# Sliding-window attention and a gated layer on one core: the branch around the fast path removed, q and k loaded ahead of the weights, another planned order

## The chip, the cores and the metric

One core of a Trainium2 chip runs the whole program. The metric is the device time of one execution in microseconds (us); the median of several runs counts, lower is better.

## The reference

```
scores = q @ k^T / sqrt(64)                      # 4 batches, 8 heads, 768 positions, head width 64
keep   = (key < n_sink) | (0 <= query - key < window)      # n_sink 4, window 128
a      = softmax(where(keep, scores, -1e9))
x      = (a @ v), heads side by side             # 3072 x 512
h      = x @ w_in                                # 512 x 2048
out    = (h * cos(h)) @ w_out                    # 2048 x 512, result 3072 x 512
```

q, k and v are fp32. The two weights come as fp64; the kernel turns each into two fp32r parts (`hi` and `lo`) and multiplies with both. `n_sink` and `window` are inputs of 64 bits, read at run time.

## The kernel before

The 3072 tokens are 12 chunks of 256 (`NT`); a chunk is two blocks of 128 queries. For each chunk and head, `banded_path` computes scores against the block before, the own block and eight sink columns, masks them (`mask`, L811), takes exponentials (`expo`, L820), normalises (`norm`, L840), transposes (`turn`, L900) and multiplies by v (`values`, L954). Pairs of heads are then split into `xhi` and `xlo` (`split_x`; the subtraction for `xlo` is L333). The dense part (`dense`) goes over each chunk in 8 slots of 256 of the 2048 columns: 24 matmuls into `h` (L372), the gate h*cos(h) on ACT and DVE (the last product is L399), its split into `ghi` and `glo` (L405, L411), and 12 matmuls into two accumulators (L420). The first three chunks (the first 256 tokens of three batches) need no sinks and take a shorter way for the attention, with q and k turned on PE (`pe_turn`, L708) into `tqe` and `tk`.

A weight arrives in 32 pieces of 128 x 512 fp64 (512 KB) through two buffers `raw`. `weight_piece` makes fp32 of each in three integer steps on DVE (L473, L479, L485), rounds it on ACT to the `hi` part (L506) and subtracts for the `lo` part on DVE or POOL (L509). Much later each piece is loaded again and `check_piece` notes whether any weight was too small for this way.

The order of the work is not written by hand. `Plan` collects steps with the engines that can do them, their dependencies, an estimated duration and a due time; `order` plays them through and appends each step to the list of the engine that is free first, and the lists are emitted as they stand. The table `C` holds the offsets of the due times (`WI`, `WO` for weights, `DQ` for q and k, `TH` for the first heads, and so on) and the handicaps with which DVE, POOL and ACT compete for the steps that several can do (`ALT`, `POOLPEN`, `POOLF`). `FILL` are 60 matmuls (L1194) without a use, put where PE has nothing due.

At the start, `setup` loads the two limits to all 128 partitions (`nw_i`, L231 and L232, on SP's queue), makes the identity, 11 warm-up products and, on DVE, both the two limits as floats (`neg`) and a `flag` that says whether they suit the banded path. The steps that the plan puts before `GATE` (5.4 us) are emitted there too. Then every engine loads `flag` and branches (L1391, L1392); inside the branch DVE makes the masks (L1244 to L1252) and the rest of the plan follows. After it the check is reduced on DVE, PE and DVE (L1262 to L1266) into `redo`, and every engine loads `redo` (L1395) and branches around the general path (L1396), which does the whole computation again when `redo` is set.

Of the kernel before, what the change touches and what calls it, by code (L numbers as in the profile page):

```python
# [27 lines left out]
    "ALT": 2.669, "BLF": -0.052, "CK": 27.435, "DA": -3.097, "DH": -2.747, "DM": -0.791, "DQ": 10.525, "DS": -2.397,  # L28
    "DV": 4.41, "DX": 7.018, "FILL": 60, "GHI": 2, "GLO": 2, "L": 1, "LAG": 4.21, "LEAD": 18.263, "NEH": 24,
    "NM": 1.373, "NW": 2.093, "NWF": 0.026, "PB": 5, "PEN": 10.744, "PL": 3, "POOLF": 0.675, "POOLPEN": 2.303,  # L30
    "PRE": 4.5, "R": 2, "RAW": 2, "SAME": 0.13, "SEM": 0.2, "SPE": 0.3, "STEP": 5.59, "T": 6.142, "TH": -1.227,
    "WARM": 11, "WI": -18.566, "WO": 7.302, "WS": 1.56, "WS2": -0.177, "WT": 2, "XV": 2,
}
GATE = 5.4
# [12 lines left out]
class Plan:  # L47
# [5 lines left out]
    def __init__(self):  # L53
        self.steps, self.bufs, self.port, self.ahead = [], {}, set(), set()
# [6 lines left out]
    def add(self, engines, fn, deps, prio, lat=0.0, table=None, port=False, ahead=False):  # L61
        self.steps.append((engines, fn, deps, prio, lat, table))
        if ahead:
            self.ahead.add(len(self.steps) - 1)
        if port:
            self.port.add(len(self.steps) - 1)
        return len(self.steps) - 1

    def order(self, gate=0.0):
# [21 lines left out]
        free = dict.fromkeys(ready, gate)  # L91
        free["SP"] = min(gate, 0.9)
        free["DVE"] = free["ACT"] = min(gate, C["PRE"])
# [8 lines left out]
        while left:  # L102
# [4 lines left out]
            for e, rs in ready.items():  # L107
# [3 lines left out]
                for i in rs:  # L111
                    engines, _, _, prio, _, tab = steps[i]
                    if now < gate - 1e-6 and e != "SP" and i not in self.ahead:
                        continue
# [53 lines left out]
        early = gate - 1e-6  # L168
        return [s for s in starts if s[0] < early], [s for s in starts if s[0] >= early]
# [3 lines left out]
def attn_moe_kernel(ctx, tc, q, k, v, n_sink, window, w_in, w_out, out):  # L173
# [46 lines left out]
    nw_i = cp.tile([P, 2, 2], I32, name="nw_i")  # L220
    nw4 = cp.tile([P, 2, 2], F32, name="nw4")
    neg3 = cp.tile([P, 3], F32, name="neg")
    neg, quarter = neg3[:, 0:2], neg3[:, 2:3]
    flag = cp.tile([1, 4], F32, name="flag")
# [4 lines left out]
    def setup():  # L229

        nc.sync.dma_start(out=nw_i[:, 0, :], in_=n_sink.unsqueeze(0).broadcast_to([P, 2]))  # L231
        nc.sync.dma_start(out=nw_i[:, 1, :], in_=window.unsqueeze(0).broadcast_to([P, 2]))  # L232
# [7 lines left out]
        nc.gpsimd.memset(redo, 1)  # L240
        nc.gpsimd.memset(xb, 0.0)

        with tc.tile_pool(name="warm", bufs=1, space=PSUM) as pool:
            warm = pool.tile([P, P], F32, name="warm")
            for _ in range(C["WARM"]):
                nc.tensor.matmul(out=warm, lhsT=ident, rhs=ident, start=True, stop=True)
# [7 lines left out]
        nc.vector.tensor_copy(out=nw4, in_=nw_i)  # L254
        nc.vector.tensor_tensor(out=lims[:, 0], in0=nw4[0:1], in1=lims[:, 0], op=ALU.is_ge)
        nc.vector.tensor_tensor(out=lims[:, 1], in0=nw4[0:1], in1=lims[:, 1], op=ALU.is_le)
        nc.vector.tensor_single_scalar(out=neg, in_=nw4[:, :, 0], scalar=0.0, op=ALU.is_lt)
        nc.vector.tensor_tensor(out=lims[:, 0], in0=lims[:, 0], in1=lims[:, 1], op=ALU.mult)
        nw_hi = nw4[:, :, 1]
        nc.vector.tensor_tensor(out=nw_hi, in0=nw_hi, in1=neg, op=ALU.add)  # L260
        nc.vector.tensor_reduce(
            out=flag[:, 0:1], in_=lims[:, 0].rearrange("p a b -> p (a b)"), axis=mybir.AxisListType.X, op=ALU.min
        )
        nc.vector.scalar_tensor_tensor(
            out=neg, in0=nw_hi, scalar=4294967296.0, in1=nw4[:, :, 0], op0=ALU.mult, op1=ALU.add
        )
        nc.vector.tensor_copy(out=flag.bitcast(I32)[:, 1:2], in_=flag[:, 0:1])
# [184 lines left out]
    def weight_piece(plan, prio, hi, lo, src, guard, first=False):  # L452
# [7 lines left out]
        else:  # L460
# [6 lines left out]
            last = add(dma(1), load, [r], -1000.0 if first else prio - C["LEAD"], lat=3.3)  # L467
# [27 lines left out]
            s1 = add((("DVE", dve(WP, True)),), shift, [last, bt], prio, port=True, ahead=True)  # L495
            s2 = add((("DVE", dve(WP)),), top, [s1], prio, port=True, ahead=True)
            s3 = add((("DVE", dve(WP)),), low, [s2], prio, port=True, ahead=True)
# [13 lines left out]
        s4 = add((("ACT", act(WP)),), round_hi, [last], prio, ahead=True)  # L511
# [74 lines left out]
    def emit(steps, before=None):  # L586
        with tc.manual_schedule():
            if before:
                before()
            for _, _, fn, e in steps:  # L590
                fn(engines[e])

    def banded_path():
# [126 lines left out]
        def early_tiles(e):  # L720
            env.tqe = ap.tile([P, 2, NT], F32, name="tqe", tag="plo")
            env.vp = [
                ap.tile([P, CB, 2 * D], F32, name="vpe", tag="vr"),
                xp.tile([P, CB, 2 * D], F32, name="vpo", tag="x", bufs=1),
            ]
            for odd in range(2):
                e.memset(env.tqe[64 - odd * 64 : 128 - odd * 64, odd], 0.0)
            e.memset(env.vp[0][:, :, D:], 0.0)
            e.memset(env.vp[1][:, :, :D], 0.0)
# [244 lines left out]
        blank = add([("POOL", 1.2)], early_tiles, early, 0.0)  # L974
        env.minus, bgt = buf("gt", 1), buf("gt", 1)
        bgt.users.append(add([("POOL", 0.4)], lambda e: e.memset(f32(gt), 0.0), [bgt], 0.0))
# [16 lines left out]
        def before_softmax(g, o):  # L993
            nonlocal first, vs_last
            t = head_time(g)
            if o.i0 == CB and o.h == 0:
                first = o
                bx, o.bt, btb, o.bv, o.bvs = buf("xq", 1), buf("ts", 1), buf("tk", 1), buf("xb", 1), buf("vs", 1)
# [5 lines left out]
                o.vt = add([("DVE", 1.1)], vs_parts(o), [i, o.bvs], t - T + 3.4, port=True)  # L1004
# [8 lines left out]
            if o.early:  # L1013
                if o.odd == 0:
                    bx, bb, o.btq = buf("xq", 1), buf("b3", 1), buf("tqe", 1)
                    src = lambda c: q[o.b, o.h + c, o.i0 * P : o.i0 * P + NT, :]
                    i = add(dma(2), load_natural(xq_t, src, CB), [bx], t - 8 * T + C["DQ"] + 0.4, lat=2.3)
# [13 lines left out]
                    i = add(dma(2), load_natural(xk_t, src, o.nkb), [bx], t - 7 * T + C["DQ"] + 1.2, lat=2.4)  # L1031
# [84 lines left out]
        def after_softmax(g, o):  # L1116
# [4 lines left out]
                dma(1), load_v(o), [bx] + ([blank] if o.early else []), t - 2 * T + C["DV"] + 3.2, lat=2.4  # L1121
# [88 lines left out]
        for m, (t, (ready, ss), piece) in enumerate(sorted(pieces, key=lambda w: w[0])):  # L1210
            i = weight_piece(plan, t, *piece, guard=False, first=m < C["PL"])
# [13 lines left out]
        nh = 0  # L1225
        for t, a, s in slots:
            hs = ("b4", "b2") if a < NE - 1 else ("b4", "b2", "b3")
# [5 lines left out]
        assert len(checked) == len(checks)  # L1233

        first_loads, steps = plan.order(GATE)
        emit(first_loads, setup)
        yield
# [5 lines left out]
        with tc.manual_schedule():  # L1243
            nc.vector.tensor_scalar(out=prev, in0=rel, scalar1=float(P), scalar2=wd_f, op0=ALU.add, op1=ALU.is_lt)  # L1244
            nc.vector.tensor_scalar(out=diag, in0=rel, scalar1=wd_f, scalar2=None, op0=ALU.is_lt)
            nc.vector.scalar_tensor_tensor(out=diag, in0=rel, scalar=0.0, in1=diag, op0=ALU.is_ge, op1=ALU.mult)
# [145 lines left out]
    with tc.If(banded > 0):  # L1392
        with ExitStack() as ctx2:
            next(fast)
# [35 lines left out]
```

## Time and profile before

| | us |
|---|---|
| median of 3 runs | 759.07 (758.25 to 761.2) |
| profiled execution: its own time | 757.07 |
| its span, first to last instruction | 755.2 |
| PE busy | 727.7 (96%) |
| DVE busy | 609.5 (81%) |
| ACT busy | 567.1 (75%) |
| POOL busy | 160.0 (21%) |

PE is the matrix engine, DVE the vector engine, ACT the scalar engine, POOL the GpSimd engine, SP the engine whose queue issues transfers. A busy share is a mean over the whole span. A line such as L372 is a line of the kernel before.

### The profile page before, as it was taken

How to read it: one execution, taken by the hardware profiler on the slowest of the kernel's cores; microseconds unless marked ns; L12 is line 12 of the kernel's file. 1: busy time of each engine (PE TensorE's matmuls, PEld its weight loads, DVE VectorE, ACT ScalarE, POOL GpSimd, SP SyncE). 2: the span in 40 equal slices, each digit the busy share in tenths (PEclk: the TensorE clock that was granted, in tenths of full speed). 3: DMA queues.
4: the chain of work that ended last, by engine and by line, in shares of the span. 5: the costliest groups of instructions: out<-in, count | busy, mean ns of one | idle time of the engine just before them, and what ended most of it. 6: DMA issues, size and time to landing. Idle time of an engine off the chain costs nothing.

```text
span 755.2 us, 15272 instructions
## 1 busy us (share of the span) xinstructions
PE 727.7 (96%) x4975; PEld 663.9 (88%) x4975; DVE 609.5 (81%) x1591; ACT 567.1 (75%) x1326; POOL 160.0 (21%) x246
## 2 busy tenths in 40 slices
PE   7779999999999999999999999999999999999996
PEld 7668888899899999999999989999999999999994
DVE  4889989868899898889989888888788998964432
ACT  2879884978868868788788787788798788784332
POOL 3210101310212243342222322221211131120000
PEclk8999999999999999999999999999999999999999
DMA  5675664322653574474475333232233233110000
GB/s 148 165 196 168 174 174 152 79 48 34 144 146 78 107 199 104 96 194 110 85 186 132 65 90 65 37 69 47 50 73 64 50 73 56 27 39 2 29 1 33
DMA packets 215673, 71.50 MB, mean 95 GB/s; under 512 B 204320, under 2 KB 204320, under 8 KB 215584
## 3 DMA queue, kind: packets, MB, share of 16 engines
q1 hardware_dynamic: 215584, 70.43, 39.1%
q8 instruction: 41, 0.67, 0.4%
q14 instruction: 48, 0.39, 0.2%
HBM read 64.10 MB, written 6.29 MB: 93 GB/s over the span
## 4 chain that ended last, share of the span: by engine, by line
PE 82%; DVE 7%; DMA 5%; ACT 3%; issue 1%; SPq 1%; DVEq 0%; ACTq 0%
PE h L372 32%; PE acc L420 31%; PE av L954 5%; PE tp L900 5%; PE s L798 4%; DMA raw<-in_moe_w_out_dram 1%; DMA xq<-in_q_dram 1%; DMA raw<-in_moe_w_in_dram 1%; PE av L930 1%; PE s L742 1%; PE gp L882 1%; ACT p L820 1%; DVE wt L479 1%; DVE wt L473 1%; DVE wt L485 1%
## 5 line engine op out<-in xcount | busy, mean ns | idle before, releaser
L372 PE MATMUL h<-xhi,whi_in 128*128 128x256 f32 x768 | 224.3, 292 | 0.0
L372 PE MATMUL h<-xlo,whi_in 128*128 128x256 f32 x768 | 216.9, 282 | 0.0
L372 PE MATMUL h<-xhi,wlo_in 128*128 128x256 f32 x768 | 216.7, 282 | 0.0
L420 PE MATMUL acc<-whi_out,ghi 128*128 128x512 f32 x384 | 156.2, 407 | 0.6 <-ACT raw L361 0.6
L372 PEld LDWEIGHTS h<-xhi,whi_in 128*128 128x128 f32 x768 | 145.9, 190 | 8.7 <-issue 0.3
L372 PEld LDWEIGHTS h<-xhi,wlo_in 128*128 128x128 f32 x768 | 146.0, 190 | 7.4
L420 PE MATMUL acc<-wlo_out,ghi 128*128 128x512 f32 x384 | 151.7, 395 | 0.1
L420 PE MATMUL acc<-whi_out,glo 128*128 128x512 f32 x384 | 150.6, 392 | 0.0
L372 PEld LDWEIGHTS h<-xlo,whi_in 128*128 128x128 f32 x768 | 145.8, 190 | 0.0
L811 DVE CUSTOM_DVE_ANT_0 p<-s,mk 128x264 f32<-128x264 f32 (+1 forms) x192 | 76.6, 399 | 27.7 <-PE s L798 20.9
L820 ACT ACTIVATE p<-p,st 128x264 f32<-128x264 f32 (+1 forms) x192 | 93.2, 487 | 0.6
L420 PEld LDWEIGHTS acc<-whi_out,glo 128*128 128x128 f32 x384 | 72.1, 188 | 16.4
L405 ACT CAST ghi<-r 128x512 fp32r<-128x512 f32 x96 | 59.2, 617 | 35.6 <-PE acc L420 33.5
L394 ACT ACTIVATE r<-r,neg 128x512 f32<-128x512 f32 x96 | 68.9, 723 | 21.7 <-DVE r L387 19.4
L420 PEld LDWEIGHTS acc<-whi_out,ghi 128*128 128x128 f32 x384 | 72.5, 189 | 5.4 <-ACT raw L361 0.8
L420 PEld LDWEIGHTS acc<-wlo_out,ghi 128*128 128x128 f32 x384 | 72.9, 190 | 5.0 <-DVE wlo_out L509 0.7
L411 DVE TENSOR_TENSOR glo<-r,ghi 128x512 fp32r<-128x512 f32 x76 | 54.9, 722 | 27.6 <-ACT ghi L405 26.8
L399 DVE TENSOR_TENSOR r<-h,r 128x512 f32<-128x512 f32 x96 | 65.0, 680 | 10.4 <-ACT r L394 10.2
L387 DVE SCALAR_TENSOR_TENSOR r<-h,yt 128x512 f32<-128x512 f32 x96 | 65.6, 683 | 5.6 <-ACT yt L381 3.3
L381 ACT ACTIVATE yt<-h 128x512 int32<-128x512 f32 x96 | 57.2, 595 | 10.6 <-PE h L372 9.4
L853 POOL TENSOR_TENSOR vr<-v,vr 128x192 fp32r<-128x192 f32 (+1 forms) x55 | 32.2, 586 | 144.8 <-ACT vr L848 132.6
L840 POOL TENSOR_SCALAR p<-p,st 128x264 f32<-128x264 f32 (+2 forms) x62 | 33.3, 550 | 139.0 <-DVE st L830 125.3
(132 smaller groups left out, 1405.0 us busy)
## 6 DMA issues: line engine op xcount, KB each, us to landing
raw<-in_moe_w_in_dram SPq DMA_DIRECT2D x32, 512.0 KB
raw<-in_moe_w_out_dram SPq DMA_DIRECT2D x32, 512.0 KB
xk<-in_k_dram SPq DMA_DIRECT2D x256, 48.0 KB
v<-in_v_dram SPq DMA_DIRECT2D x64, 96.0 KB
out_dram<-raw SPq DMA_DIRECT2D x24, 256.0 KB
xq<-in_q_dram SPq DMA_DIRECT2D x144, 32.0 KB
xq<-in_q_dram SPq DMA_DIRECT2D x24, 64.0 KB
xk<-in_k_dram SPq DMA_DIRECT2D x24, 64.0 KB
```

The source lines that it names most:

```text
L372: nc.tensor.matmul(out=o.h[:, t, :], lhsT=w[:, c, fs], rhs=xx[:, c, :], start=(c == 0 and n == 0), stop=(c == NC - 1 and n == 2),)
L381: nc.scalar.activation(out=yt, in_=o.h, func=AF.Copy, scale=INV2PI, bias=0.25)
L387: nc.vector.scalar_tensor_tensor(out=o.r, in0=o.h, scalar=INV2PI, in1=yt, op0=ALU.mult, op1=ALU.subtract)
L394: nc.scalar.activation(out=o.r, in_=o.r, func=AF.Sin, scale=TWOPI_DOWN, bias=quarter)
L399: nc.vector.tensor_tensor(out=o.r, in0=o.h, in1=o.r, op=ALU.mult)
L405: nc.scalar.copy(out=o.ghi, in_=o.r)
L411: e.tensor_tensor(out=o.glo, in0=o.r, in1=f32(o.ghi), op=ALU.subtract)
L420: nc.tensor.matmul(out=x.acc[j], lhsT=gg[:, t, j * P : (j + 1) * P], rhs=w[:, f, :], start=(f == 0 and n == 0), stop=(f == NFT - 1 and n = ...
L811: nc.vector.tensor_tensor_reduce(out=o.p[:, j, :w], in0=o.s_ps[j][:, :w], in1=masks[min(o.i0 + j, 2)][:, :w], op0=ALU.add, op1=ALU.min, sc ...
L820: nc.scalar.activation(out=o.p[:, j, :w], in_=o.p[:, j, :w], func=AF.Exp, bias=o.lead.st[:, 0, o.nth, j : j + 1], scale=-1.0, accum_out=o. ...
L900: nc.tensor.transpose(out=o.tp[:, n * P : (n + 1) * P], in_=o.p[:, i - o.i0, c0 : c0 + P], identity=ident)
L954: nc.tensor.matmul(out=dst, lhsT=lhs, rhs=rhs, start=(n == 0), stop=(n == len(seq) - 1), skip_group_check=True)
```

## The change

The branch on `flag` goes. The plan is one list again (`GATE`, `PRE` and the steps marked as ahead are gone), and the engines' first free times in it are five new numbers (`P0` to `S0`). The limits are loaded by ACT's queue into one partition, four steps there make them floats, and one product of a row of ones with them (`both`) puts them on 128 partitions; `neg` is copied from it. The test of the limits moves to `limits`, part of the step `again`, which stands in the plan near the end, takes in the reduced check and writes `redo`. The loads of the first q and k get due times ahead of the first weight pieces. The clears of `vs` and `gc` become steps of the plan. The table has new values throughout, so that the planner makes another order and another share-out between engines; the steps themselves are the same.

```diff
 C = {
-    "ALT": 2.669, "BLF": -0.052, "CK": 27.435, "DA": -3.097, "DH": -2.747, "DM": -0.791, "DQ": 10.525, "DS": -2.397,
...
+    "ALT": 2.676, "BLF": -0.126, "CK": 45.236, "DA": -4.303, "DH": -1.332, "DM": -0.747, "DQ": 9.553, "DS": -2.337,
...
-GATE = 5.4
...
-        nc.sync.dma_start(out=nw_i[:, 0, :], in_=n_sink.unsqueeze(0).broadcast_to([P, 2]))
-        nc.sync.dma_start(out=nw_i[:, 1, :], in_=window.unsqueeze(0).broadcast_to([P, 2]))
+        nc.scalar.dma_start(out=nw_i[:, 0, :], in_=n_sink.unsqueeze(0))
+        nc.scalar.dma_start(out=nw_i[:, 1, :], in_=window.unsqueeze(0))
...
+            for _ in range(C["WARM"]):
+                nc.tensor.matmul(out=warm, lhsT=ident, rhs=ident, start=True, stop=True)
+
+            nc.vector.tensor_copy(out=nw4, in_=nw_i)
+            nc.vector.tensor_single_scalar(out=low, in_=nw4[:, :, 0], scalar=0.0, op=ALU.is_lt)
+            nc.vector.tensor_tensor(out=low, in0=nw4[:, :, 1], in1=low, op=ALU.add)
+            nc.vector.scalar_tensor_tensor(
+                out=low, in0=low, scalar=4294967296.0, in1=nw4[:, :, 0], op0=ALU.mult, op1=ALU.add
+            )
+            nc.tensor.matmul(out=both, lhsT=ones, rhs=low, start=True, stop=True)
...
+            nc.vector.tensor_copy(out=neg, in_=both)
...
-            last = add(dma(1), load, [r], -1000.0 if first else prio - C["LEAD"], lat=3.3)
+            last = add(dma(1), load, [r], first if first else prio - C["LEAD"], lat=3.3)
...
+                    pq = t - 8 * T + C["DQ"] + 0.4 if g else C["LD"] - 2
+                    i = add(dma(2), load_natural(xq_t, src, CB), [bx], pq, lat=2.3)
...
+        def again(e):
+            limits()
...
+            nc.vector.scalar_tensor_tensor(
+                out=redo, in0=tmin[0:1, 1:2], scalar=-MIN_TOP * MIN_TOP, in1=flag, op0=ALU.is_gt, op1=ALU.max
+            )
...
-    fast = banded_path()
-    next(fast)
-    banded = nc.values_load(flag.bitcast(I32)[:, 1:2], min_val=0, max_val=1)
-    with tc.If(banded > 0):
-        with ExitStack() as ctx2:
-            next(fast)
+    with ExitStack() as ctx2:
+        banded_path(ctx2)
     again = nc.values_load(redo, min_val=0, max_val=1)
```

SP's list at the start, before (`nw_i` are the limits, `raw` the weight buffers, `xq` and `xk` those of q and k, `xb` and `v` those of v):

```order
L231 DMA nw_i<-in_n_sink_dram 128x2
L232 DMA nw_i<-in_window_dram 128x2
L465 DMA raw_70<-in_moe_w_in_dram 128x1024
L465 DMA raw_71<-in_moe_w_in_dram 128x1024
L700 DMA xq<-in_q_dram 128x2x64 x2
L700 DMA xk<-in_k_dram 128x2x64 x2
L635 DMA xb<-in_v_dram 8x4x64 x4
L1391 TENSOR_LOAD flag
```

SP's list at the start with the change:

```order
L701 DMA xq<-in_q_dram 128x2x64 x2
L701 DMA xk<-in_k_dram 128x2x64 x2
L468 DMA raw_70<-in_moe_w_in_dram 128x1024
L468 DMA raw_71<-in_moe_w_in_dram 128x1024
L682 DMA vpe<-in_v_dram 128x2x64
L682 DMA vpo<-in_v_dram 128x2x64
L636 DMA xb<-in_v_dram 8x4x64 x4
```

The limits have left SP's queue, q and k stand first, and no branch follows.

DVE's list with the change, from the limits to the first masked score (`sm` holds the limits as floats, `both` is the product, `mk` the masks; L814 and L476 to L488 are L811 and L473 to L485 before):

```order
L255 SCALAR_TENSOR_TENSOR sm<-sm 1x2
L261 COPY neg<-both 128x2
L1291 TENSOR_SCALAR mk<-yt,neg 128x128
...
L1299 TENSOR_SCALAR mk<-mk 128x648
L476 TENSOR_SCALAR wt_72<-raw_70 128x512
L814 ISA p_0_0_201,st_0_0_202<-s_0_0_0_196,mk 128x128
L814 ISA st_0_0_202 128x1
L482 SCALAR_TENSOR_TENSOR wt_72<-raw_70,wt_72 128x512
```

Before, the masks' nine steps stood behind the branch and among three steps of two weight pieces; now they are in a row, and one weight step stands between them and the first masked score.

SP's list at the end with the change:

```order
L682 DMA v_1_77<-in_v_dram 128x3x64
L1424 TENSOR_LOAD redo
L1424 ISA x2
L439 DMA out_dram<-raw_70 128x512
L439 DMA out_dram<-raw_71 128x512
L439 DMA out_dram<-raw_70 128x512
L439 DMA out_dram<-raw_71 128x512
L1425 COMPARE_AND_BRANCH
```

Before, the load of `redo` and its branch stood behind the last store and the end of the first branch's body; now the load is ahead of the last four stores.

## Rows read from the trace of the kernel before

**Rows 1.** The page: span, and PE's busy time, share and instructions.

```profile
span 755.2 us, 15272 instructions
...
PE 727.7 (96%) x4975; PEld 663.9 (88%) x4975; DVE 609.5 (81%) x1591; ACT 567.1 (75%) x1326; POOL 160.0 (21%) x246
```

**Rows 2.** Windows: from:to, length, busy us of each engine, clock, DMA share, GB/s.

```profile
0.00:15.15 15.15, 10.23 (x48) 10.07 (x49) 6.49 (x30) 2.90 (x5) 5.30 (x17) 0.79 0.46 123
...
60.00:100.00 40.00, 36.06 (x240) 32.05 (x239) 37.85 (x86) 37.24 (x88) 4.82 (x5) 1.00 0.61 170
0.00:100.00 100.00, 83.11 (x517) 73.53 (x518) 81.64 (x233) 73.14 (x197) 18.69 (x31) 0.95 0.61 169
100.00:150.00 50.00, 48.77 (x317) 43.84 (x316) 45.44 (x100) 37.22 (x80) 11.42 (x13) 1.00 0.48 134
...
100.00:745.00 645.00, 641.68 (x4448) 588.26 (x4447) 527.44 (x1357) 492.75 (x1128) 141.33 (x215) 1.00 0.37 84
745.00:755.20 10.20, 2.95 (x14) 2.11 (x12) 0.42 (x2) 1.17 (x2) 0.00 (x0) 0.89 0.18 61
```

**Rows 3.** Timeline of SP's queue: start, issue time, line, transfer.

```profile
1.18 0.42 SPq L232 DMA_DIRECT2D nw_i<-in_window_dram  x1
1.65 0.90 SPq L465 DMA_DIRECT2D raw<-in_moe_w_in_dram  x2
```

**Rows 4.** Timeline of DVE, first 16 us: start, duration, line, instruction, what it waited for.

```profile
6.00 0.17 DVE L254 CAST nw<-nw_i 128x4 f32<-128x4 int32 x1 [3.84 <-DMA nw_i<-in_window_dram]
...
7.51 0.43 DVE L473 TENSOR_SCALAR wt<-raw 128x512 int32<-128x512 int32 x1 [0.55 <-DMA raw<-in_moe_w_in_dram]
...
9.66 0.53 DVE L1244 TENSOR_SCALAR mk<-yt,neg 128x128 f32<-128x128 f32 x1 [0.31 <-DVE wt L473]
...
13.10 0.50 DVE L1252 TENSOR_SCALAR mk<-mk 128x648 f32<-128x648 f32 x1
15.15 0.29 DVE L811 CUSTOM_DVE_ANT_0 p<-s,mk 128x128 f32<-128x128 f32 x1 [1.56 <-PE s L742]
```

**Rows 5.** Timeline of PE, first 20 us: q's turn, first scores, ten fillers.

```profile
9.55 0.66 PE L708 MATMUL qk<-ident,xq 128*128 128x128 f32 x2 [3.56 <-DMA xq<-in_q_dram]
...
14.49 1.38 PE L742 MATMUL s<-tk,tqe 128*128 128x128 f32 x4
...
17.67 1.43 PE L1194 MATMUL idle<-gt 128*128 128x256 f32 x10
```

**Rows 6.** The end: last stores, window of 0.5 us, the SP queue's own waits.

```profile
747.13 1.69 SPq L436 DMA_DIRECT2D out_dram<-raw  x2
...
750.00:750.50 0.50, 0.00 (x0) 0.00 (x0) 0.00 (x0) 0.00 (x0) 0.00 (x0) 1.00 0.45 107
...
SPq L1396 <- SPq L1396: 3.1, 1, 3.1
SPq L1425 <- PEq L1425: 0.6, 2, 0.5
```

**Rows 7.** Groups by line on DVE: busy us, mean ns, idle before and its releasers.

```profile
L411 DVE TENSOR_TENSOR glo<-r,ghi 128x512 fp32r<-128x512 f32 x76 | 54.9, 722 | 27.6 <-ACT ghi L405 26.8
...
L840 DVE TENSOR_SCALAR p<-p,st 128x264 f32<-128x264 f32 (+2 forms) x80 | 30.0, 428 | 0.5
...
L333 DVE TENSOR_TENSOR xlo<-x,xhi 128x256 fp32r<-128x256 f32 x15 | 8.0, 533 | 1.3 <-ACT xhi L316 1.3
L509 DVE TENSOR_TENSOR wlo_in<-wt,whi_in 128x512 fp32r<-128x512 f32 x11 | 7.5, 683 | 0.9 <-ACT whi_in L506 0.8
```

**Rows 8.** Timelines of DVE and POOL around 44 us.

```profile
44.35 1.41 DVE L473 TENSOR_SCALAR wt<-raw 128x512 int32<-128x512 int32 x1 [0.99 <-DMA raw<-in_moe_w_in_dram]
...
44.21 1.26 POOL L509 TENSOR_TENSOR wlo_in<-wt,whi_in 128x512 fp32r<-128x512 f32 x1 [2.47 <-ACT whi_in L506]
```

**Rows 9.** Timeline of DVE: the gate steps of the sixth and thirteenth slot.

```profile
96.82 0.68 DVE L399 TENSOR_TENSOR r<-h,r 128x512 f32<-128x512 f32 x1
...
151.08 0.68 DVE L399 TENSOR_TENSOR r<-h,r 128x512 f32<-128x512 f32 x1
```

More of the change, by code (lines that the diff above doesn't have):

```diff
@@ L53, in __init__ @@
     def __init__(self):
-        self.steps, self.bufs, self.port, self.ahead = [], {}, set(), set()
+        self.steps, self.bufs, self.port = [], {}, set()
     def buf(self, tag, n):
@@ L59, in buf, with add @@
         return row[-1]
-    def add(self, engines, fn, deps, prio, lat=0.0, table=None, port=False, ahead=False):
+    def add(self, engines, fn, deps, prio, lat=0.0, table=None, port=False):
         self.steps.append((engines, fn, deps, prio, lat, table))
-        if ahead:
-            self.ahead.add(len(self.steps) - 1)
         if port:
@@ L67, in add, with order @@
         return len(self.steps) - 1
-    def order(self, gate=0.0):
+    def order(self, late=False):
         steps = self.steps
@@ L90, in order @@
         ready = {e: set() for e in ("PE", "ACT", "POOL", "DVE", "SP")}
-        free = dict.fromkeys(ready, gate)
-        free["SP"] = min(gate, 0.9)
-        free["DVE"] = free["ACT"] = min(gate, C["PRE"])
+        free = dict.fromkeys(ready, 0.0)
+        if late:
+            free.update(PE=C["P0"], ACT=C["A0"], DVE=C["D0"], POOL=C["G0"], SP=C["S0"])
         events = [(0.0, i) for i in range(n) if not wait[i]]
@@ L167, in order @@
                 now = wake[0]
-        early = gate - 1e-6
-        return [s for s in starts if s[0] < early], [s for s in starts if s[0] >= early]
+        return starts
 @with_exitstack
@@ L239, in setup @@
         nc.gpsimd.iota(rc_i[:, 1], pattern=[[1, P]], base=0, channel_multiplier=0)
-        nc.gpsimd.memset(redo, 1)
         nc.gpsimd.memset(xb, 0.0)
[L243 to L246, printed above, removed]
+        nc.vector.memset(ones, 1.0)
         nc.vector.memset(quarter, HALF_PI_DOWN)
@@ L253, in setup, with limits @@
         nc.vector.tensor_copy(out=rc, in_=rc_i)
[L254 to L260, printed above, removed]
+        with tc.tile_pool(name="warm", bufs=1, space=PSUM) as pool:
+            warm = pool.tile([P, P], F32, name="warm")
+            both = pool.tile([P, 2], F32, name="both")
+            for _ in range(C["WARM"]):
[7 more added lines that the diff above has]
+            nc.tensor.matmul(out=both, lhsT=ones, rhs=low, start=True, stop=True)
+            for _ in range(C["WARM2"]):
+                nc.tensor.matmul(out=warm, lhsT=ident, rhs=ident, start=True, stop=True)
+            nc.vector.tensor_copy(out=neg, in_=both)
+    def limits():
+        nc.vector.tensor_tensor(out=lims[:, 0], in0=nw4, in1=lims[:, 0], op=ALU.is_lt)
+        nc.vector.tensor_tensor(out=lims[:, 1], in0=nw4, in1=lims[:, 1], op=ALU.is_gt)
+        nc.vector.tensor_tensor(out=lims[:, 0], in0=lims[:, 0], in1=lims[:, 1], op=ALU.max)
         nc.vector.tensor_reduce(
-            out=flag[:, 0:1], in_=lims[:, 0].rearrange("p a b -> p (a b)"), axis=mybir.AxisListType.X, op=ALU.min
+            out=flag, in_=lims[:, 0].rearrange("p a b -> p (a b)"), axis=mybir.AxisListType.X, op=ALU.max
         )
[L264 to L267, printed above, removed]
     ns_f = neg[:, 0:1]
@@ L509, in rest_lo @@
             e.tensor_tensor(out=lo, in0=t32, in1=f32(hi), op=ALU.subtract)
-        s4 = add((("ACT", act(WP)),), round_hi, [last], prio, ahead=True)
+        s4 = add((("ACT", act(WP)),), round_hi, [last], prio)
         s5 = add(sub(WP), rest_lo, [s4], prio, port=True)
@@ L1003, in before_softmax @@
                 i = add(dma(4), load_batch_v(o), [o.bv], t - 3 * T, lat=2.3)
-                o.vt = add([("DVE", 1.1)], vs_parts(o), [i, o.bvs], t - T + 3.4, port=True)
+                d = [i, o.bvs]
+                held.append(d)
+                o.vt = add([("DVE", 1.5)], vs_parts(o), d, t - T + 3.4, port=True)
                 o.bv.users.append(o.vt)
@@ L1271, in banded_path @@
-        yield
+        for _, _, fn, e in steps:
+            fn(engines[e])
     def general_path():
@@ L1286, in general_path @@
         }
-        emit(plan.order()[1])
+        emit(plan.order())
         for a, (b, i0) in enumerate(chunks):
```

123 lines of the change are left out of this document (69 added, 54 removed).

## The prediction, made before the result was known

> **What bounds the kernel now.** I read the page first, then the windows by stage, then the timeline of the first 16 us engine by engine, the last 10 us, and last the groups of instructions that the change moves. The page [rows 1] shows PE busy 96% of the 755.2 us span. The windows [rows 2] say where the rest lies: from 100 to 745 us PE misses 645 - 641.68 = 3.3 us in all, and from 745 us on 10.20 - 2.95 = 7.3 us. The first 100 us miss 16.9 us, and there PE also runs 60 filler matmuls and 11 warm-up products that compute nothing. So the kernel is PE-bound in its long middle part, and can win only at its two ends, unless the middle gets worse.
>
> **The start.** SP issues the two limits, two weight pieces, then q and k [rows 3]. The limits' second transfer, issued at 1.18, releases DVE at 6.00 [rows 4], 4.8 us later; each limit goes to 128 partitions. PE gets q at 9.55 and its first scores at 14.49 [rows 5]. On DVE the mask steps begin at 9.66, behind the branch, and the last one starts at 13.10; the first masked score is at 15.15 [rows 4]. Up to there DVE was busy 6.49 us of 15.15 [rows 2], so idle 8.7.
>
> **The end.** The second of SP's last two stores is issued at about 748.4 (747.13 + 1.69 less 0.4 for its own issue), and the transfers are over in the window that begins at 750.0 [rows 6]; so a store takes 1.9 us. The span ends 4.9 us after 750.3. The queue's own waits there are 3.1 us on SP's own L1396, the branch over the general path, and 0.6 us in two pieces on L1425 [rows 6]; what is left, some 1.2 us, I read as the wait for all transfers, the load of `redo` and the compare, which stand in SP's order behind the last store.
>
> **The sum is made against** the profiled execution's own 757.07 us (span 755.2 and 1.9 around it), which is 2.0 us under the median of the runs, 759.07. I add those 2.0 at the end. A measurement of this kernel can tell about 0.5% (3.8 us) from no change.
>
> **The change, part by part.**
>
> *End: -2.5.* In the new order SP loads `redo` ahead of the last stores and has the compare right behind them, and the two steps that reduce the check stand before the last slots on DVE. The 1.9 us of the last store now lie beside the branch's 3.1, and the load and exit (some 0.6 of the 1.2) go. Bounds: 0, if the exit waits for the stores before it branches, and -3.7 (all of 1.9, 1.2 and 0.6). I take 1.9 + 0.6.
>
> *Start: -4.* First the chain. The limits go out on ACT's queue, the second at about 1.2, one partition each. The trace has no transfer that small; bounds are 4.8 us [rows 4] and 1.9 us (the store). I take 2.1, near the store, because the 128 targets are gone: landed at 3.3. Four steps on DVE, each about 0.1 us behind the one before, make 3.7; the product and the copy 0.6 more: 4.3. The nine mask steps took 13.10 + 0.50 - 9.66 = 3.9 us with three weight steps of 0.6 between them, so 2.1 without: 6.4. On PE the product at 4.0, 18 fillers at 0.14 each [rows 5] and the two turns of q and k put the first scores at about 7.5, if q and k, now first in SP's order, have landed by 4.6. DVE's first masked score stands behind the first step on a weight piece, whose transfer is issued at about 2.6 instead of 1.65 and took until 7.51 before [rows 4]; so about 8.2 for 15.15, 6.9 us earlier. DVE has done less by then (about 4.5 us of work for 6.49, as the two weight pieces are not yet begun), so its idle time falls from 8.7 to 3.7: 5.0 us saved. From there to 100 us DVE is nearly full (81.64 - 6.49 = 75.2 busy of 84.85) [rows 2], so it is DVE's work that paces PE until PE has a stock. Up to the sixth gate step L399, at 96.82 [rows 9], the new order has 2 `glo` and 4 `wlo` more on DVE (4.2 us at the means of [rows 7]), and 4 weight steps, 2 masks and 4 sink steps fewer: about 1 us less. So the sixth gate comes some 6 us earlier. Up to the thirteenth, at 151.08, it has 8 us more than before (4 `glo`, 8 `wlo`, 4 other steps of 2 us, less 6 `p` of 0.43); that is 9 us more between the two gates, against DVE's idle 50 - 45.44 = 4.6 us there [rows 2]. Of the 4.4 not covered I let half, 2, come through to PE. Hence -6 + 2 = -4. Bounds: -6.9 (the whole head start is kept) and -1.6 (all 4.4 comes through).
>
> *Middle: 0.* The new order takes work from POOL: on DVE's list there are 96 `glo` for 76, 30 `xlo` for 15, 31 `wlo` for 23, and 71 `p` for 80. At the means of [rows 7] that is 20 x 0.722 + 15 x 0.533 + 8 x 0.683 - 9 x 0.428 = 14.4 + 8.0 + 5.5 - 3.9 = 24 us more on DVE. From 100 to 745 us DVE is idle 645 - 527.44 = 117.6 us [rows 2], which covers it five times over, and nothing of it is a result that PE waits for on average; bounds are -3.3, all the idle time PE has left there, and +12, half of the 24 us. PE itself has the same matmuls in both orders.
>
> A row speaks for a lower price of the moved work. One weight step on DVE that takes 0.43 us at 7.51 [rows 4] took 1.41, from 44.35 to 45.76, while a subtraction on POOL ran from 44.21 to 45.47 [rows 8]: DVE stood until POOL was done. The Trainium skill, page "SBUF — State Buffer", section "Who interferes with whom", has this as a rule: the port pair that DVE and GpSimd share is an exclusive lock, held for a whole instruction. By that rule the 43 subtractions that leave POOL also stop blocking DVE, and the 24 us would be an upper price; by the rows alone it is 24, and the sum takes 0 in either case.
>
> *At nothing:* 5 warm-up products for 11 (PE idles there anyway); the two issues gone from SP (0.8 us, inside the head start); the clears of `vs` and `gc`, which POOL makes later, between two steps of its own that wait for DVE anyway.
>
> Sum: 757.07 - 2.5 - 4.0 + 0 = 750.6; with the 2.0 us to the median, **752.6 us**.
>
> **The rivals.**
>
> 1. *The head start is swallowed.* DVE's 9 us more between the sixth and thirteenth gates come through in full, and more idle time behind the first scores eats the rest: start 0, end -2.5: 756.6. For it speaks that DVE is busy 37.85 of the 40 us from 60 to 100 [rows 2]; against it that PE hardly waits after 100 us, when DVE still had idle time. Chance 0.15.
>
> 2. *The limits land late.* By the 4.8 us of [rows 4], now from 1.2 on: landed at 6.0, masks ready at 9.1 for 6.4, 2.7 us later; PE, too, stands behind the product, and the fillers are queued behind it. Start -1.3, so 755.3. The Trainium skill, page "SBUF — State Buffer", section "Can I just issue two DMAs to hit both halves?", says that issuing from several engines does not help, since all transfers share the same 16 engines. By that rule the other queue alone brings nothing, and only the single partition can. For it: q, k and weights are in flight at once. Against it: q and k are issued about when the limits are, not 1 MB of weights. Chance 0.12.
>
> 3. *DVE becomes the bound in the middle: slower.* Place: `glo`, `xlo` and the masks in the slots after 100 us. It decides if DVE's idle time there is mostly waiting on ACT and PE, which cannot be filled. Then a us more on DVE is a us on PE, and if more than 6.5 of the 24 come through, the kernel is slower; with all but the start's share, say 18, it is 757.07 - 6.5 + 18 + 2 = 770.6. Against it: 117.6 us of idle, and the same `wlo` subtraction takes POOL 1.26 us [rows 8] and DVE 0.683 [rows 7], so what waits on a moved one waits less. Chance 0.08.
>
> 4. *All of it is kept:* start -6.9, end -2.5, and 2 of PE's 3.3 us in the middle go too: 747.7. For it: weights are asked for earlier, and POOL blocks DVE less. Chance 0.17.
>
> That the change does not do what it says is hardly open: the branch is gone from every engine's list, and q and k stand first on SP's.
>
> **How the numbers follow.** The forecast has 0.48, with its own range from 749 to 755. Faster by over 0.5% means under 755.3: 0.46 of the forecast, all of rival 4, 0.07 of rival 2: 0.70. Slower means over 762.9: rival 3 and a rest, 0.09. Within 0.5%: 0.21. The range takes in rivals 4, 2 and 1 and leaves out rival 3 and the extremes: from 745 (all lower bounds at once give 757.07 - 3.7 - 6.9 - 3.3 + 2.0 = 745.2) to 757.5.
>
> **What would show it.** Right, if DVE's first masked score is near 8.2 (under 9), PE's first scores near 7.5, the sixth gate near 91, the last store issued some 4 us earlier, and the span ends about 2.4 us after that store has landed. Rival 2 shows as a first mask step after 6.5; rival 1 as PE idle of 17 us or more in the first 100 us; rival 3 as PE idle well over 3.3 us after 100 us, released by DVE. A tail as long as before, or more than 8 us of new PE idle in the middle, would make the prediction wrong.

## The result, and the profile after

The changed kernel takes 746.67 us (median of 4 runs, 746.09 to 748.58) against 759.73 beside it: ratio 0.9831, interval 0.9808 to 0.9853. In a later job, with its own variants around it, it took 748.49 against 759.64: 0.9861, 0.9840 to 0.9881. So it is faster by 11 to 13 us. The two profiled executions are 9.9 us apart in span, because the profiled execution of before lies below the median of its runs.

The page of the changed kernel, for [rows 1]:

```profile
span 745.3 us, 15192 instructions
...
PE 725.2 (97%) x4965; PEld 660.8 (89%) x4965; DVE 614.6 (82%) x1637; ACT 555.6 (75%) x1319; POOL 112.1 (15%) x201
```

The windows by stage, for [rows 2]; columns as there:

```profile
0.00:10.15 10.15, 8.54 (x37) 8.23 (x38) 4.31 (x24) 2.39 (x4) 2.32 (x13) 1.00 0.60 161
60.00:100.00 40.00, 37.92 (x257) 34.08 (x254) 38.88 (x97) 34.05 (x88) 4.35 (x7) 1.00 0.65 182
0.00:100.00 100.00, 88.34 (x557) 77.75 (x557) 86.88 (x248) 76.53 (x208) 10.25 (x25) 0.98 0.65 180
100.00:150.00 50.00, 49.08 (x319) 44.78 (x320) 45.00 (x103) 35.69 (x79) 3.30 (x9) 1.00 0.43 116
100.00:735.00 635.00, 632.72 (x4391) 579.95 (x4392) 527.74 (x1390) 477.89 (x1110) 101.83 (x177) 1.00 0.37 83
735.00:745.30 10.30, 4.16 (x19) 3.11 (x17) 0.00 (x0) 1.17 (x2) 0.00 (x0) 0.94 0.17 59
```

PE's idle time in the first 100 us falls from 16.9 to 11.7 us. Of its busy time there the warm-up takes 2.5 us for 4.6, and the 60 fillers take 11.8 in both; so PE has done 7.3 us more of useful work by 100 us. In the middle PE misses 2.3 us for 3.3. The tail is 1.2 us shorter (below). Together that is 7.3 + 1.0 + 1.2 = 9.5 of the 9.9; the other 0.4 is PE's busy time on the same useful products, which differs by that much between the two executions.

The start, for [rows 3 to 5]: the cast of the limits and the first masked score on DVE; on PE the product, the fillers behind q's turn, and the first scores:

```profile
2.66 0.22 DVE L252 CAST sm<-nw_i 1x4 f32<-1x4 int32 x1 [0.55 <-DMA nw_i<-in_window_dram]
...
10.15 0.29 DVE L814 CUSTOM_DVE_ANT_0 p<-s,mk 128x128 f32<-128x128 f32 x1 [2.63 <-PE s L745]
```

```profile
3.79 0.58 PE L258 MATMUL both<-sm,wt 1*128 1x2 f32 x2
...
5.92 1.84 PE L1213 MATMUL idle<-gt 128*128 128x256 f32 x7
...
9.48 1.21 PE L745 MATMUL s<-tk,tqe 128*128 128x128 f32 x4
```

DVE has its masks early, then waits 2.63 us for PE, and PE is at fillers, 0.26 us each. The first masked score comes 5.0 us sooner than at 15.15. The sixth and thirteenth gates, for [rows 9]:

```profile
87.42 0.67 DVE L402 TENSOR_TENSOR r<-h,r 128x512 f32<-128x512 f32 x1
...
146.25 0.69 DVE L402 TENSOR_TENSOR r<-h,r 128x512 f32<-128x512 f32 x1
```

They are 9.4 and 4.8 us sooner. A single gate is a rough measure, though: the eleventh is 3.4 us sooner and the twelfth 9. The twelfth, before and with the change:

```profile
146.84 0.68 DVE L399 TENSOR_TENSOR r<-h,r 128x512 f32<-128x512 f32 x1
```

```profile
137.79 0.69 DVE L402 TENSOR_TENSOR r<-h,r 128x512 f32<-128x512 f32 x1
```

The end, for [rows 6]: SP's last two stores, and two windows of half a microsecond:

```profile
738.45 1.69 SPq L439 DMA_DIRECT2D out_dram<-raw  x2
```

```profile
741.00:741.50 0.50, 0.00 (x0) 0.00 (x0) 0.00 (x0) 0.00 (x0) 0.00 (x0) 1.00 0.67 234
741.50:742.00 0.50, 0.00 (x0) 0.00 (x0) 0.00 (x0) 0.00 (x0) 0.00 (x0) 1.00 0.16 41
```

SP's load of `redo` and its branch over the general path in the kernel before (durations in ns, then the first and the last start in us):

```profile
L1395 SPq TENSOR_LOAD <-redo x1: 727/727/727, 749.1 to 749.1; - x1
L1396 SPq COMPARE_BRANCH  x1: 45/45/45, 749.9 to 749.9; - x1
```

The branch with the change, and what SP does next:

```profile
L1425 SPq COMPARE_BRANCH  x1: 45/45/45, 740.2 to 740.2; - x1
L1425 SPq EVENT_SEMAPHORE  x8: 17/17/17, 743.4 to 743.9; - x8
```

With the change SP comes to the branch at 740.2, as soon as the last store is issued (738.45 + 1.69 = 740.14), and goes on at 743.4. The stores are over by about 742, so they land beside the branch. Before, the load of `redo` stood between the last issue and the branch, and SP came to the branch at 749.9; the stores were over only by about 750.5 [rows 6], so there, too, they landed in part beside the branch. From the start of the last stores' issue to the branch it is 1.75 us for 2.8 before, from the branch to the end 5.1 for 5.3, in all 6.85 for 755.2 - 747.13 = 8.07.

DVE's groups that grew or got cheaper, for [rows 7]:

```profile
L414 DVE TENSOR_TENSOR glo<-r,ghi 128x512 fp32r<-128x512 f32 x96 | 66.3, 691 | 31.6 <-ACT ghi L408 31.2
...
L476 DVE TENSOR_SCALAR wt<-raw 128x512 int32<-128x512 int32 x32 | 13.5, 421 | 2.3 <-DMA raw<-in_moe_w_in_dram 2.1 <-DMA raw<-in_moe_w_out_dram 0.2
L336 DVE TENSOR_TENSOR xlo<-x,xhi 128x256 fp32r<-128x256 f32 x30 | 13.4, 446 | 1.1 <-ACT xhi L319 1.0
```

### The profile page after: what moved, and what is told of

Its sections match the earlier page's. It is cut to its first block, busy times and chain, and to the rows that moved or that the text cites. A ratio compares the mean times of both kernels' runs of the same rounds, so it can differ in the third digit from the quotient of the medians.

```text
span 745.3 us, 15192 instructions
## 1 busy us (share of the span) xinstructions
PE 725.2 (97%) x4965; PEld 660.8 (89%) x4965; DVE 614.6 (82%) x1637; ACT 555.6 (75%) x1319; POOL 112.1 (15%) x201
## 4 chain that ended last, share of the span: by engine, by line
PE 86%; DVE 6%; DMA 3%; ACT 3%; issue 1%; SPq 0%; POOL 0%; DVEq 0%; POOLq 0%; ACTq 0%
PE h L375 33%; PE acc L423 33%; PE av L957 5%; PE tp L903 5%; PE s L801 4%; DMA raw<-in_moe_w_in_dram 2%; PE av L933 2%; PE s L745 1%; PE idle L1213 1%; DMA xk<-in_k_dram 1%; PE gp L885 1%; DVE p L814 1%; DVE wt L482 1%; ACT p L841 1%; DVE wlo_in L512 1%
## 5 line engine op out<-in xcount | busy, mean ns | idle before, releaser
L814 DVE CUSTOM_DVE_ANT_0 p<-s,mk 128x264 f32<-128x264 f32 (+1 forms) x192 | 76.7, 400 | 23.2 <-PE s L801 17.3
L414 DVE TENSOR_TENSOR glo<-r,ghi 128x512 fp32r<-128x512 f32 x96 | 66.3, 691 | 31.6 <-ACT ghi L408 31.2
L843 POOL TENSOR_SCALAR p<-p,st 128x264 f32<-128x264 f32 (+2 forms) x70 | 36.1, 530 | 236.8 <-DVE st L833 202.5
L856 POOL TENSOR_TENSOR vr<-v,vr 128x192 fp32r<-128x192 f32 (+1 forms) x57 | 35.5, 623 | 183.4 <-ACT vr L851 148.0
```

The lines of the kernel that those rows point to most:

```text
L414: e.tensor_tensor(out=o.glo, in0=o.r, in1=f32(o.ghi), op=ALU.subtract)
L814: nc.vector.tensor_tensor_reduce(out=o.p[:, j, :w], in0=o.s_ps[j][:, :w], in1=masks[min(o.i0 + j, 2)][:, :w], op0=ALU.add, op1=ALU.min, sc ...
```

## The experiments

Every ratio is to the kernel before, run in the same job; 0.001 is 0.76 us.

**A later start in the same order.** Two kernels put more warm-up products ahead of the product of the limits, in an order otherwise the same.

```diff
-"WARM": 5,
+"WARM": 17,      (warm29: 29)
```

> The changed kernel with 17 warm-up products instead of 5, nothing else. They stand ahead of the product that spreads the limits; before, 11 of them took 4.63 us, so 12 more put everything behind the product (masks, fillers, scores) about 5.0 us later, in the same order. Theory A (the head start at the beginning passes to the end in full): 746.7 + 5.0 = 751.7. Theory B (the head start is mostly swallowed by DVE's work up to the thirteenth gate, the gain comes from the new order): under +2, at most 748.7.

> The changed kernel with 29 warm-up products instead of 5: 24 more, about 10.1 us later in the same order. Theory A: 756.8, a straight line through the 17 of the other run. Theory B: under +4, at most 750.7.

Measured: warm17 0.9855 (0.9833 to 0.9877), warm29 0.9886 (0.9867 to 0.9906). That is 1.8 and 4.2 us above the changed kernel's first ratio, 0.7 and 3.0 above the mean of its two. The doses were smaller than meant: the first masked score came 2.1 and 4.8 us later, for behind more warm-up products the fillers ran at 0.15 us each. The sixth gate came about 2.8 and 6.9 us later, the end of the profiled span 2.0 and 7.4 (warm29's profiled execution is the slowest of its six). The two doses against each other, in one job, are the cleanest pair: a start 2.7 us later makes a median 2.4 us later (750.28 and 752.69, each known to about 1.6). So in this order most of a late start seems to reach the end, as theory A had it.

**Structure and table apart.** `old_numbers` is the changed code with the old table (but 5 warm-up products, and with the numbers that only the new table has), `new_numbers` the code before with the new table (but 11). Six of the values that `old_numbers` puts back:

```diff
 C = {
-    "DA": -4.303, "DS": -2.337, "DV": 5.777, "DX": 5.639, "LEAD": 26.374, "WI": -20.327,
+    "DA": -3.097, "DS": -2.397, "DV": 4.41, "DX": 7.018, "LEAD": 18.263, "WI": -18.566,
...
```

> The changed kernel (no branch around the banded path, limits through ACT's queue and the product, q and k first, check ahead of the last slots), but with the old values of the table in all entries that both have, except the number of warm-up products. So the planner shares out and orders the work nearly as before, with the head start kept. Theory A (head start kept, order neutral): 746.7 within 2. The prediction's own sum (order neutral, 2 us given back) has 753. Theory B (the new order is what gains): 754 or more.

> The kernel before with the new table for every number that both tables have; the branch, the limits to 128 partitions ahead of the weights, q and k behind the weights, 11 warm-up products and the check at the end stay. Theory A (the new order hands a late or early start through one to one, as the warm-up doses showed): about 5 us of late first scores and 1.2 us of tail on top of the changed kernel, 753, ratio 0.990 to 0.994, the sixth gate about 5 us later than the changed kernel's 87.4. Theory B (the order alone is the gain, the start matters little): under 750, ratio under 0.986. Theory C (the order needs the early start, whose times its numbers were chosen for): 757 or more, ratio over 0.997.

| ratio to before | old numbers | new numbers |
|---|---|---|
| code before | 1 | 1.0008 (0.9989 to 1.0027) |
| changed code | 0.9961 (0.9941 to 0.9981) | 0.9831 and 0.9861 |

The changed code alone brings 3 us (1.4 to 4.5 by the interval) and takes 758.47 us, as theory B had it (754 or more); the table alone brings nothing, as theory C had it; together they bring 11 to 13. But each cell is one planned order, and the neighbours below show that a near order can cost 5 to 7 us. So the table does not show that code and numbers need each other. The old numbers in the changed code show one way in which a head start goes. Their first masked score is at 9.17, a microsecond ahead of the changed kernel, and their sixth gate at 96.12, where it was before. The window from 60 to 100 us, and DVE's waits from 55 to 125 us (engine, line, what for: us, times, longest):

```profile
60.00:100.00 40.00, 34.43 (x204) 30.14 (x203) 32.70 (x78) 29.72 (x71) 8.81 (x9) 0.91 0.55 161
```

```profile
DVE wt L475 <- DMA raw<-in_moe_w_out_dram: 3.4, 3, 1.2
...
DVE wt L475 <- DMA raw<-in_moe_w_in_dram: 1.2, 1, 1.2
```

DVE is busy 32.70 us there, 38.88 in the changed kernel, and waits 4.6 us for weights. PE falls behind too: from 70 to 75 us it is busy 2.59 us, and of the ten that follow a good part runs at 1.2 for 2.4 GHz (granted mean 0.66; 60 to 100 us in the changed kernel 1.00):

```profile
75.00:85.00 10.00, 9.22 (x45) 8.36 (x46) 7.71 (x17) 5.32 (x13) 2.17 (x2) 0.66 0.58 171
```

How much of the loss is the waits and how much PE's slower pace was not separated. In the changed kernel, whose `LEAD` is 8 us larger, the same wait for weights is one of 0.2 us:

```profile
DVE wt L476 <- DMA raw<-in_moe_w_out_dram: 0.2, 1, 0.2
```

`new_numbers` does not wait for weights there either, and its start is as late as before (first masked score at 15.31, sixth gate at 96.84); so weights in time are not enough by themselves.

**The branch alone.** The kernel before without the branch on `flag`, and so without the test of the limits.

```diff
-    banded = nc.values_load(flag.bitcast(I32)[:, 1:2], min_val=0, max_val=1)
-    with tc.If(banded > 0):
-        with ExitStack() as ctx2:
-            next(fast)
+    with ExitStack() as ctx2:
+        next(fast)
```

> The kernel before with only the branch on flag taken out (the limits' test is left out with it); limits, q and k, weights and the table of numbers as before. The load of redo then also has no end of a branch body before it. Theory A: what the branch held up at the start is small, since DVE sat 0.3 us before the first mask step and PE waited for q: 1 us there and 1.2 us at the end, 757.5. Theory B says the same; a rival C, that the branch itself was the cost (engines held up until the limits have landed and every engine has loaded the flag), has 752 or less.

Measured: 1.0008 (0.9989 to 1.0028), so none of the three theories' gains shows. The first masked score came 0.8 us sooner, the first six gates 1.5 to 1.8, the seventh at 109.01 for 108.97. The head start goes in twelve products into the accumulators ahead of the seventh gate. Before, then without the branch, from the chain that ended last, and the window without the branch:

```profile
96.57 2.76 PE acc L420 x12
```

```profile
95.03 4.34 PE acc L420 x12
```

```profile
95.00:100.00 5.00, 5.00 (x20) 4.09 (x19) 3.45 (x9) 4.16 (x14) 0.00 (x0) 0.66 0.57 159
```

They begin 1.5 us sooner and take 1.6 us longer, because PE, which had been busy only 2.74 of the five us before, runs for a part of them at the lower level; in the kernel before the granted clock is 1.00 there. So nothing of the branch reaches the end, within 0.2%, and the profiled execution lost its head start to PE's pace; whether every execution does, the runs do not tell.

**q and k.** In `qk_behind` the first q and k get due times behind the first weight pieces (k's line is changed in the same way), and the plan is made anew. In `qk_swap` the changed kernel's plan is kept, and only on SP's list the two loads change places with the two pieces.

```diff
-pq = ... if g else C["LD"] - 2
+pq = ... if g else C["LD"] + 1
```

> The changed kernel with the first q and k issued behind the first two weight pieces, as before. Theory A (q and k ahead of the weights is what makes the first scores early, and the gates follow): q lands some 3 to 4 us later (9 for 5.6), first scores near 13, every gate and the end 3 to 4 us later, 750 to 751, ratio 0.988. Theory B (only DVE's work paces the first 100 us, and the weights come 1 us sooner for it): first scores late, but the sixth gate within 1 us of 87.4 and the end within 1 us of the changed kernel.

```diff
-        steps = plan.order(True)
+        steps = list(plan.order(True))
+        sp = [j for j, s in enumerate(steps) if s[3] == "SP"][:4]
+        for j, s in zip(sp, [steps[j] for j in sp[2:] + sp[:2]]):
+            steps[j] = s
```

> The changed kernel with its planned order kept step for step on every engine; only on SP's list the first two weight pieces change places with the loads of the first q and k. Theory A (in a fixed order a late start is handed on about one to one): with q and k behind the weights the limits were cast 1.3 us later and the first masked score came 1.2 us later; so 1 to 2 us above the changed kernel, 748 to 749, ratio 0.984 to 0.987, sixth gate at 88 to 89. Theory E (the ten us lost with q and k behind come from the transfers themselves, which then collide in the first 100 us): 5 us or more above, ratio 0.990 or more, sixth gate over 95. If A holds, the rest of those ten came from planning anew around the moved loads.

Measured: `qk_behind` 0.9963 (0.9948 to 0.9978), `qk_swap` 0.9883 (0.9861 to 0.9904), in whose job the changed kernel had 0.9861. The start is late alike in both. First masked score of `qk_behind`, then of `qk_swap`, for 10.15:

```profile
11.30 0.29 DVE L814 CUSTOM_DVE_ANT_0 p<-s,mk 128x128 f32<-128x128 f32 x1 [1.00 <-PE s L745]
```

```profile
11.33 0.29 DVE L814 CUSTOM_DVE_ANT_0 p<-s,mk 128x128 f32<-128x128 f32 x1 [3.04 <-PE s L745]
```

In the kept order that costs 1.4 us at the sixth gate (88.84) and 1.7 at the end by the ratios (2.5 by the medians), as theory A had it. In the new plan the sixth gate comes at 99.06, 11.6 us later than in the changed kernel. So the transfers' order is worth some 2 us, and some 6 us of `qk_behind` come with the plan that the planner made around the moved loads. Neither of the two theories stated for `qk_behind` held.

**Neighbours of both orders.** Four due times (`DA`, `DS`, `DV`, `DX`) are moved by about 0.1 us: `nudge` and `nudge_back` from the changed kernel's table, one each way, `nudge_before` from the table before.

```diff
-"DA": -4.303, "DS": -2.337, "DV": 5.777, "DX": 5.639
+"DA": -4.2, "DS": -2.25, "DV": 5.9, "DX": 5.5
```

> The changed kernel with four due times in the table moved by about 0.1 us (DA, DS, DV, DX), a control for how much any new order costs. Theory A (the gain comes from the early start and large offsets such as weights asked for earlier): within 1.5 us of the changed kernel, ratio 0.981 to 0.985. Theory D (the table was found by search, and any other order, however near, loses): 3 us or more above it, ratio 0.987 or more.

> The changed kernel with the same four due times moved by about 0.1 us the other way. Theory D (the order is a found one, its neighbours are worse): 3 us or more above the changed kernel, ratio 0.987 or more, although the start and the sixth gate are as early. Theory A (gain by large offsets and the early start alone, the first nudge a mishap): ratio 0.981 to 0.985.

> The kernel before with those four due times moved by about 0.1 us. If its order, too, is a found one and both kernels stand at the best of their neighbourhood: 3 to 6 us above the kernel before, ratio 1.004 to 1.008, and the 13 us between the two compare like with like. If only the changed kernel's order is a lucky one: within 0.2% of the kernel before, and 6 of the 13 us come from that order, not from the early start.

> The changed kernel as it is, once more, beside its own variants: ratio 0.981 to 0.985, as measured first. With the check behind everything the ratio was 0.987, 3 us more, of which the tail shows 0.9; if this run comes out at 749 to 750, the rest of those 3 us is the spread between jobs, if at 746 to 747, the check's place costs more than the tail shows.

Measured: `nudge` 0.9908 (0.9886 to 0.9931), `nudge_back` 0.9937 (0.9919 to 0.9956), `nudge_before` 1.0020 (1.0005 to 1.0034), the changed kernel again 0.9861. Against the mean of the changed kernel's two ratios, 0.9846, its neighbours lose 4.7 and 6.9 us, as theory D had it; that of the kernel before loses 1.5, just within the 0.2% of the second reading stated for it. The changed kernel came out a little above the 0.981 to 0.985 expected. The two neighbours lose in different places. Windows of `nudge`, then of `nudge_back`:

```profile
0.00:100.00 100.00, 88.71 (x560) 77.43 (x561) 87.36 (x252) 78.01 (x212) 10.87 (x25) 0.98 0.66 184
...
250.00:450.00 200.00, 196.83 (x1377) 178.71 (x1377) 180.17 (x493) 160.61 (x378) 39.83 (x66) 1.00 0.51 125
```

```profile
100.00:150.00 50.00, 45.79 (x288) 40.57 (x288) 45.84 (x107) 36.39 (x81) 3.42 (x6) 1.00 0.46 125
```

`nudge` keeps the start (88.71 for 88.34 us of PE in the first 100) and loses 2.7 us of PE from 250 to 450 us, where the changed kernel has 199.56; `nudge_back` loses 3.3 between 100 and 150, and its sixth gate, at 90.23, is 2.8 us late already. Three neighbours are a small sample: of the 11 to 13 us some 5 to 7 hang on this one order, and 5 to 7 are left with the nudged ones, which have the early start and the large offsets.

**The check at the end.** The changed kernel with the reduced check and `redo` behind all planned steps.

```diff
-        t, bt = slot_time(len(chunks) - 1, 0), buf("tp", 1)
-        i = add([("DVE", 0.2)], least, checked, t) if checks else None
-        i = add([("PE", 0.11)], least_turn, [i, bt], t) if checks else None
-        add([("DVE", 0.7)], again, [i] if checks else [], t)
...
         for _, _, fn, e in steps:
             fn(engines[e])
+        if checks:
+            least(None)
+            least_turn(None)
+        again(None)
```

> The changed kernel with the reduced check and the write of redo behind all planned steps on each engine, as before; everything else as changed. If the new place of the check is worth the 1.2 us by which the tail shrank, 1.2 us more than the changed kernel, about 748, and 6.8 us from the issue of the last store to the end; if it is worth the 2.5 predicted, about 749; if nothing, the same as the changed kernel with 5.6 us from the last store to the end.

Measured: 0.9869 (0.9851 to 0.9887), and from the last stores' issue at 740.61 to the end at 748.3 it takes 7.69 us, 0.84 more than the changed kernel and 0.4 less than before. The tail lies between those expected, 1.2 longer or as in the changed kernel. The load of `redo` stands behind the last store again, and SP comes to the branch 2.6 us after the stores' issue begins, for 1.75 in the changed kernel:

```profile
L1424 SPq COMPARE_BRANCH  x1: 45/45/45, 743.2 to 743.2; - x1
```

The ratio agrees with that beside the changed kernel's second one, 0.9861; against its first, 0.9831, 2 us would stay unexplained, which the spread between jobs covers.

## Why the prediction came out as it did

The direction and the range (745 to 757.5) held, at the low end; the likeliest time, 752.6, was 4 to 6 us too high. Nearest came rival 4, all of the head start kept, at 747.7. Of the signs that the prediction named for being right, the first scores (9.48 for 7.5), the first masked score (10.15, not under 9) and the end of the span 2.4 us after the last store (more than 3) did not come; the sixth gate was sooner than the 91 it named. So the range held in part by luck: of the way from the one profiled execution to the other, the sum took 1.3 us too much at the end and 4.3 too little at the start and in the middle.

*End: predicted -2.5, measured -1.2.* The step that failed: "The 1.9 us of the last store now lie beside the branch's 3.1, and the load and exit (some 0.6 of the 1.2) go." The sum had the store, the load of `redo` and the branch one behind the other. They were not: before, the load ran from 749.1 on while the last store was still landing, and SP came to the branch at 749.9, ahead of the landing at about 750.5. So only what stood between the issue of the last store (over at 748.82) and the branch could go, 1.1 us; with the change it is under 0.1. `check_last`, which puts the load back there, loses 0.84 of the 1.2. The bound of 0, an exit that waits for the stores before it branches, is not what happened.

*Start: predicted -4 (-6 at the sixth gate, 2 given back), measured -7.3 by PE's work in the first 100 us.* It was made of two errors against each other. The first scores were to come at 7.5 and the first masked score at 8.2; they came at 9.48 and 10.15. The limits were even sooner than taken (cast at 2.66 for 3.3). What failed was "18 fillers at 0.14 each": 14 of them took 3.7 us, 0.26 each. The price was taken from a row at 17.67; the trace of before had the dearer one, 0.24, in the very place, behind the turns, where the granted clock from 10 to 15 us was 0.50:

```profile
11.36 3.33 PE L1194 MATMUL idle<-gt 128*128 128x256 f32 x14
```

But the sixth gate came 9.4 us sooner and not 6, although DVE began only 5.0 sooner: between first masked score and sixth gate it took 77.3 us for 81.7. It was fuller, 38.88 for 37.85 us from 60 to 100. Between the sixth and the thirteenth gate 4.6 us were given back, which looks like the 4.4 of the sum but is not: the twelfth gate is 9 us sooner, and DVE did 4.6 us more there and not 9, with as much idle time as before (5.1 us). The stretch between the two gates, before and with the change:

```profile
96.82:151.08 54.26, 53.03 (x338) 47.49 (x338) 49.11 (x110) 41.07 (x92) 11.42 (x13) 1.00 0.48 129
```

```profile
87.42:146.25 58.83, 56.30 (x366) 50.95 (x365) 53.72 (x125) 43.90 (x104) 4.49 (x9) 1.00 0.50 136
```

"Of the 4.4 not covered I let half, 2, come through to PE" is the term that was mis-sized: nothing came through. PE was busy 49.08 of the 50 us from 100 to 150 (48.77 before), with other work than that of the gates. A gate's time is not PE's time.

*Middle: predicted 0 at 24 us more on DVE, measured -1.0 at 5.1 us more.* The rows of the groups with moved steps rise by 18.5 us (66.3 - 54.9 for `glo`, 5.4 for `xlo`, 4.8 for `wlo`, -3.1 for `p`), for the 24 at the old means. All of DVE's groups together rise by less, some 12 us, because steps that did not move take less: the first weight step 421 ns for 505 in the mean. DVE's busy time rises by only 5.1, since a step often begins before the one ahead of it has ended, and the rows count that time twice (the mask step at 9.87 of the trace of before begins 0.3 us ahead of the end of the one from 9.66). What makes a step cheaper shows in the shortest, median and longest of the first weight step, before and with the change:

```profile
L473 DVE TENSOR_SCALAR wt<-raw x32: 374/422/1405, 7.5 to 131.3; 128x512 int32<-128x512 int32 x32
```

```profile
L476 DVE TENSOR_SCALAR wt<-raw x32: 410/420/434, 7.1 to 124.5; 128x512 int32<-128x512 int32 x32
```

The median is the same and the long ones are gone. In the trace of before the 22 that meet no POOL step take 420 ns, none over 429, and the ten that overlap one take 692 in the mean; POOL is busy 160.0 us there and 112.1 with the change. That bears out the reading of [rows 8]. It agrees with the lock of the shared port that the Trainium skill names on the page "SBUF — State Buffer", section "Who interferes with whom". DVE becoming the bound (rival 3) did not show.

*The two us to the median:* the changed kernel's profiled execution, 747.2, lies at its median. The 2.0 were the spread of the runs before, not a constant; by the profiled executions alone the forecast of -6.5 stands against -9.9.

*What the sum had no term for.* It took the head start as the structure's, and the order as something that could only give some of it back. The runs show otherwise: the same early start under the old numbers is worth 3 us, and four due times moved by 0.1 us cost 5 to 7. The order at hand keeps DVE and ACT fed while weights arrive (waits of 0.2 us, for 4.6 under the old numbers), and what is gained at the start is still there at 100 us. Rival 1, the swallowed head start, did not come true here; it is what `old_numbers` shows, whose sixth gate is no sooner than before. Which of the table's numbers does it was not separated: weights asked for earlier fit the waits, but no run changed `LEAD` alone, and a new plan can cost 5 us or more by itself.

*What no run holds fixed.* PE's granted clock differs from plan to plan, and its share was not tested. Over the whole span, in the mean of all runs, it is 0.987 in `qk_behind` and 0.992 in `qk_swap`, 0.988 in `new_numbers` and 0.992 in the kernel before. As an estimate from these, 0.005 of 755 us is some 8 us more at 1.2 for 2.4 GHz in `qk_behind`, which can make up to 4 of its 6 us; in `new_numbers` it can make up to 3. It is not the whole of it: `nudge` has the changed kernel's 0.993 and still loses 4.7.

## What to carry to other kernels

Where a planner makes the order, a changed due time is a new order, and four due times moved by 0.1 us cost 5 to 7 us here; compare a change with the order held fixed (a swap on one list, a longer warm-up) before reading a re-planned run as the effect of what was moved, and set the granted clock of each stretch beside the two. A head start counts for what the following stage can keep: ask of every engine on the way whether its next inputs are asked for early enough. An exit that branches behind the last stores is shortened by what stands between their issue and the branch, 1.0 us here, not by the time that the stores take to land. See when a wait begins before adding it to what stands ahead of it in the list.

## What was not expected of the hardware

- The second limit was cast 1.4 us after its issue with q and k in flight (issued at 1.28, cast at 2.66), and 2.8 us after it with 1 MB of weights issued ahead of q and k (`qk_swap`, at 4.08), both times in one partition on ACT's queue. In the kernel before, 128 partitions on SP's queue ahead of the weights, it was 4.8 [rows 4]. Which share is the partitions' and which the queue's or the order's was not separated.
- The same filler matmul took 0.26 us behind 5 warm-up products and 0.15 behind 17 (7 in 1.07 us at 9.35 in `warm17`), and PE's granted clock reads 1.00, the upper level of 2.4 GHz, in both stretches. In the kernel before it took 0.24 where that clock reads 0.50. So in the first 9 us that column does not tell PE's pace; the row of a group does.
- At the jump over the general path SP's queue stands 3.0 to 3.4 us in every profile of this case, wherever the load of its condition stands. It is not the stores that it stands for: with the change POOL comes to the same branch at 684.3, more than 50 us ahead of the last store, and goes on at 687.1, 2.8 us later. What an engine does in that time the profile does not tell.
